# RetNet attention followed by a leaky-ReLU MLP: aligned tiles and a reordered first phase

## The chip, the cores and the metric

The kernel runs on one core of one Trainium2 chip. The metric is the device time of one execution in microseconds (us). The profile is one execution taken by the hardware profiler; its own times are counted from the first instruction.

## The reference

```python
# q, k, v: (8, 8, 576, 64); per head h, gamma = 1 - 2**(-5 - h)
scores = scale * np.matmul(q, k.transpose(0, 1, 3, 2))
Dmat = np.where(rel >= 0, gamma[:, None, None] ** rel[None, :, :], 0.0)   # rel = i - j
ret = np.matmul(scores * Dmat[None], v)
x = ret.transpose(0, 2, 1, 3).reshape(B * S, H * D)                        # 4608 x 512
h = x @ w_in                                                               # 512 x 2048
out = np.maximum(0.01 * h, h) @ w_out                                      # 2048 x 512
```

All inputs and the output are float32.

## The kernel before

**Tiling.** The 4608 tokens are cut into 36 units of 128 tokens, each of two chunks of 64. The attention runs in its recurrent form: for each unit, masked scores within a chunk, and a running state (k-transposed times v, summed over the chunks before) that serves all later chunks. The two wide products run over groups of 256 tokens (18 groups): a block of the first product (g1, `g1_blocks`, L408) is 8 matmuls of 128x256 into one PSUM bank and one Lrelu activation to float16 on ScalarE (L427); a block of the second (g2, `g2_blocks`, L434) is 4 matmuls of 128x512 (L443); after four of them VectorE copies the bank to `osb` (L453) and SP stores it. The first two groups' second product goes through four banks at once (`g2_wide`, L474, matmuls L488): rows n=0 and 1 in the pool `yps`, n=2 and 3 in the pool `hps`, which the first product uses too.

**A unit's steps.** `loads` (L133) brings q, k, v in float32. `casts` (L162) makes float16: k by ScalarE (L139), q and v times a decay table by VectorE or GpSimd (`scaled`, L141; VectorE for units below `NEARLY`). For units below `NPE` = 9, `transposes` (L169) turns q and k on TensorE (L179) and two copies bring them to SBUF (L185), k's on ScalarE, q's on VectorE; from unit 9 on, `cast_q` issues a DMA transpose on SP's queue (L153). `scores` (L191) computes the chunk scores (L198) and the state's increments (L207); `masks` (L214, VectorE L216) and `states` (L223, VectorE L230 to L240) follow; `state_copy` (L247, L249) makes a float16 state, by ScalarE for early units and by GpSimd after. `outputs_acc` (L257, units 0 to 3) or `outputs` (L290: ScalarE copy L319, VectorE addition L323) gives `xT`, the transposed input of the first product. `keep_warm` (L352) issues matmuls on zeros.

**Order.** The program is scheduled by hand: each engine runs its instructions in the order in which this code issues them. Up to about 68 us the order is written out line by line (L508 to L609); after that `run` (L463) spreads the `steady` steps (L372) evenly between blocks of g1 and g2. `steady(n)` does scores(n), outputs(n-1), masks(n), states(n), casts(n+3) and loads(n+5). Loads of units 0 to 11 and the weights are issued by GpSimd, which spends 0.88 us on each full load of a unit's q, k or v; the later loads, the DMA transposes from unit 9 on and the results are issued by SP, in order. `ld_pool` has five buffers for each of q, k and v, `h_pool` and `y_pool` two PSUM banks each, `sc_pool` and `ot_pool` one tile each. `sc_pool`'s tile serves scores and, from unit 4 on, the transposes.

In the written order the weights of the first product come in four quarters (two DMAs each, L337); the first block needs the first quarter.

```python
    blocks(0, 0)
    scores(3)
    outputs_acc(2)
    masks(3)
    states(3)
    blocks(0, 1)
...
    some(3, 4)
    casts(5)
    some(4, 6)
    outputs(4)
    transposes(5, sc_pool)
    some(6, 9)
    scores(5)
```

`blocks(g, fq)` is two blocks of g1; `some(a, b)` is wide blocks a to b-1 in the order part by part, n = 0 to 3 in each; `more(list, a, b)` is the same for g1[2] and g2.

Of the kernel before, what the change touches and what calls it, by code (L numbers as in the profile page):

```python
# [9 lines left out]
FP = mybir.dt.float32  # L10
F16 = mybir.dt.float16
# [6 lines left out]
def kernel(  # L18
# [23 lines left out]
    nc = tc.nc  # L42
# [3 lines left out]
    P = 128  # L46
# [26 lines left out]
    consts = np.concatenate([tab.reshape(P, -1), mask, gblk], axis=1).astype(np.float32)  # L73
# [4 lines left out]
    const_pool = ctx.enter_context(tc.tile_pool(name="const", bufs=1))  # L78
# [5 lines left out]
    sc_pool = ctx.enter_context(tc.tile_pool(name="scp", bufs=1, space=PSUM))  # L84
# [3 lines left out]

    ctx.enter_context(tc.manual_schedule())

    cs = const_pool.tile([P, consts.shape[1]], FP, name="cs")
    ident = const_pool.tile([P, P], F16, name="ident")
    nc.scalar.dma_start(out=cs, in_=c_dram.ap())
    nc.scalar.dma_start(out=ident, in_=i_dram.ap())
    tab_sb = cs[:, 0:NTAB].rearrange("p (w x h) -> p w x h", x=2, h=H)
# [7 lines left out]

    NPE = 9
    NFIRST = 8
    NEARLY = 9
    NRING = 11
    t32 = {}
    qk16 = {}
# [3 lines left out]
    st16 = {}  # L113
    st32 = {}
# [18 lines left out]
    def loads(u, eng):  # L133
        for x in (1, 0, 2):
            load(u, x, eng)
# [26 lines left out]
    def casts(u):  # L162
        if u >= NU:
            return
        cast_k(u)
        cast_q(u)
        cast_v(u)

    def transposes(u, pool=None):  # L169

        qkT[u] = b_pool.tile([P, 2, NP, P], F16, name="qkT")
        if pool is None:
            trs = [y_pool.tile([P, NP, P], F16, name="yps") for x in range(2)]
        else:
            both = pool.tile([P, 2, 2 * NP, P], F16, name="sc")
            trs = [both[:, x, 0:NP, :] for x in range(2)]
        for x in (1, 0):
            for p in range(NP):
                nc.tensor.transpose(  # L179
                    trs[x][:, p, :],  # L180
                    qk16[u][:, x, 2 * p : 2 * p + 2, :].rearrange("t h d -> t (h d)"),
                    ident,
                )
        for x in (1, 0):
            (nc.scalar.copy if x else nc.vector.tensor_copy)(  # L185
                out=qkT[u][:, x], in_=trs[x]
            )

# [34 lines left out]
    def states(u, copy=True):  # L223

        st = sc_tiles[u][:, :, 1]
        s32 = a_pool.tile([P, 2, NP, CH], FP, name="s32")
        st32[u] = s32
        for j, (b, c) in enumerate(units[u]):
            if c == CB - 1:
                nc.vector.memset(s32[:, j], 0.0)  # L230
                continue
            ends_block = c % CPB == CPB - 1
            dst = a_pool.tile([P, NP, CH], FP, name="stmp") if ends_block else s32[:, j]
            if c == 0:
                nc.vector.tensor_copy(out=dst, in_=st[:, j])
            else:
                prev = s32[:, 0] if j else st32[u - 1][:, 1]
                nc.vector.tensor_tensor(out=dst, in0=st[:, j], in1=prev, op=ADD)  # L238
            if ends_block:
                nc.vector.tensor_tensor(  # L240
                    out=s32[:, j], in0=dst,
                    in1=gblk_sb.unsqueeze(2).to_broadcast([P, NP, CH]), op=MUL,
                )
        if copy:
            state_copy(u)

    def state_copy(u):  # L247
        st16[u] = a_pool.tile([P, 2, NP, CH], F16, name="st16")
        (nc.scalar.copy if u < NEARLY else nc.gpsimd.tensor_copy)(out=st16[u], in_=st32[u])  # L249

    def st_before(u, j):

# [4 lines left out]
    def outputs_acc(u):  # L257

        ot = ot_pool.tile([P, 2, 2 * NP, CH], FP, name="ot")
        o_all = ot[:, 0].rearrange("q (c j) t -> q c j t", j=2)  # L260
        seen = set()
        for r in range(2):
            if r:
                nc.tensor.drain()
            for h in (0, 4, 1, 5, 2, 6, 3, 7):
                o, c = divmod(h, NP)
                nc.tensor.matmul(
                    out=o_all[half(o), c, r, :],
                    lhsT=v16[u][half(r), h, :],
                    rhs=s16s[u][half(r), h % 2, h // 2, :],  # L270
                    start=o not in seen, stop=False, skip_group_check=True,
                )
                seen.add(o)
            for j in range(2):
                if u == 0 and j == 0:
                    continue
                for h in (r, r + 4, r + 2, r + 6):
                    o, c = divmod(h, NP)
                    nc.tensor.matmul(
                        out=o_all[half(o), c, j, :],  # L280
                        lhsT=st_before(u, j)[half(r), h // 2, :],
                        rhs=qkT[u][half(r), 0, h // 2, half(j)],
                        start=False, stop=True, skip_group_check=True,
                    )
        t0 = P * u % XR
        nc.scalar.copy(
            out=xT[:, :, t0 : t0 + P], in_=o_all.rearrange("q c j t -> q c (j t)")
        )
# [53 lines left out]
            in_=moe_w_out[c * FQ : (c + 1) * FQ, :].rearrange("(c k) f -> k c f", k=P),  # L342
        )

    warm = const_pool.tile([P, 1], FP, name="warm")
    nc.vector.memset(warm, 0.0)
    nc.scalar.activation(out=warm, in_=warm, func=mybir.ActivationFunctionType.Lrelu)
    nc.vector.memset(zst, 0.0)
# [3 lines left out]
    def keep_warm(n):  # L352

        t = h_pool.tile([P, 1, TOK], FP, name="hps")
        for _ in range(n):
            nc.tensor.matmul(out=t[:, 0, :], lhsT=idle[:, 0:P], rhs=idle, start=True, stop=True)
# [36 lines left out]
    ends = []  # L393
# [69 lines left out]
    def run(upto, *lists):  # L463

        order = sorted(
            ((n + 0.5) / len(ls), x, n) for x, ls in enumerate(lists) for n in range(len(ls))
        )
        a = done
        for m, (_, x, n) in enumerate(order):
            lists[x][n]()  # L470
            run_steps(min(upto, a + -(-(upto - a) * (m + 1) // max(1, len(order) - 3)), done + 1))
        run_steps(upto)

    def g2_wide(tbs):  # L474


        ys = []

        def block(part, n):
            g, tb = tbs[n]  # L480
            for f in range(4 * part, 4 * part + 4):
                if f == 0:
                    ys.append(
                        y_pool.tile([P, DM], FP, name="yps")
                        if n < 2
                        else h_pool.tile([P, 1, DM], FP, name="hps")[:, 0, :]
                    )
                nc.tensor.matmul(  # L488
                    out=ys[n],
                    lhsT=g_tiles[g][:, f, tb * P : (tb + 1) * P],  # L490
                    rhs=w_out16[:, f, :],
                    start=(f == 0),
                    stop=(f == NF - 1),
                )
            if part == 3:
                osb = o_pool.tile([P, DM], FP, name="osb")
                nc.vector.tensor_copy(out=osb, in_=ys[n])  # L497
                r0 = starts[g] + tb * P
                nc.sync.dma_start(out=out[r0 : r0 + P, :], in_=osb)

        return [lambda part=part, n=n: block(part, n) for part in range(4) for n in range(4)]

    def blocks(g, *parts):
        for fq in parts:
            for m in (2 * fq, 2 * fq + 1):
                g1[g][m]()

    g1 = [g1_blocks(g) for g in range(3)]  # L508
# [11 lines left out]
    for u in (2, 3):  # L520
# [8 lines left out]
        states(u - 1)  # L529
        if u == 2:  # L530
            cast_v(3)
    blocks(0, 0)
    scores(3)
    outputs_acc(2)
    masks(3)
    states(3)
    blocks(0, 1)
    outputs_acc(3)
    blocks(0, 2)
# [1 line left out]
    loads(5, nc.gpsimd)  # L541
    for c in (2, 3):
        load_w_out(c)
    for u in range(6, NRING + 1):
        loads(u, nc.gpsimd)
    blocks(1, 1)
    blocks(1, 2)
    blocks(0, 3)
    casts(4)
    blocks(1, 3)  # L550

    wide = g2_wide([(0, 0), (0, 1), (1, 0), (1, 1)])
# [1 line left out]
    def some(a, b):  # L554
        for m in range(a, b):
            wide[m]()

    g2 = g2_blocks(2)

    def more(blocks, a, b):  # L560
        for m in range(a, b):
            blocks[m]()

    some(0, 1)
    transposes(4, sc_pool)
    some(1, 3)
    scores(4)
    masks(4)
    states(4)
    some(3, 4)  # L570
    casts(5)
    some(4, 6)
    outputs(4)
    transposes(5, sc_pool)
    some(6, 9)
    scores(5)
    masks(5)
    states(5)
    some(9, 13)
    outputs(5)  # L580
    some(13, 14)
    casts(6)
    some(14, 16)
    transposes(6, sc_pool)
    more(g1[2], 0, 2)
    scores(6)
    masks(6)
    states(6, copy=False)
    more(g1[2], 2, 3)
    state_copy(6)  # L590
    casts(7)
    more(g1[2], 3, 5)
    outputs(6)
    transposes(7, sc_pool)
    more(g1[2], 5, 7)
    scores(7)
    masks(7)
    states(7, copy=False)
    more(g1[2], 7, 8)
    more(g2, 0, 1)  # L600
    state_copy(7)
    casts(8)
    more(g2, 1, 3)
    outputs(7)
    casts(9)
    loads(12, nc.sync)
    transposes(8, sc_pool)
    casts(10)
    more(g2, 3, 4)  # L609
    run(ends[4], g1_blocks(3), g2[4:])  # L610
    for g in range(4, NG):
        run(ends[g + 1], g1_blocks(g), g2_blocks(g - 1))
    g2 = g2_blocks(NG - 1)
# [44 lines left out]
```

## Time and profile before

| what | value |
|---|---|
| runs | 308.23, 308.55, 312.86, 312.96, 314.57 us (median 312.86) |
| profiled execution | 308.23 us, span 306.3 us |
| granted TensorE clock over the span | 0.998 |
| time before the first block of the first product | 19.18 us |
| loads of q, k, v by GpSimd, by SP | 256 KB each, median 4.9 to 5.1 us and 3.4 to 4.2 us from issue to landing |
| w_in quarters | two DMAs each, 9.0 us median from issue to landing |
| DMA transposes | 27 on SP's queue, 2.8 us median to landing |

PE is TensorE, DVE VectorE, ACT ScalarE, POOL GpSimd and SP SyncE; "SPq" and "POOLq" are issues of DMAs. A timeline row has the start, the duration, the engine, the line, the operation with its output and inputs, how many instructions were merged, and in brackets how long the engine had been idle and what ended that. A stage row has the length, then busy time and instruction count for PE, PEld (weight loads), DVE, ACT and POOL, the granted clock, the DMA engines' share and GB/s. PE ends are modelled, so that neighbouring PE rows overlap by some tenths.

### The profile page before, as it was taken

Reading aid. Unit: us, or ns where it says so; the run is one execution under the profiler, and the core shown is the slowest. Engines: PE = TensorE matmul, PEld = TensorE weight load, DVE = VectorE, ACT = ScalarE, POOL = GpSimd, SP = SyncE. Lnnn points to the kernel's source line nnn. Section 1 sums busy time; section 2 is a strip of 40 time slices with the busy share of each in tenths; the row PEclk is TensorE's granted clock in tenths of the full one; section 3 lists DMA queues with packets and bytes.
Section 4 is the critical chain, followed back from the end, with each engine's and each line's share of the span. In section 5 each row is a group of like instructions: output and inputs, shape, how many; then the busy total and the mean of one; then the engine's idle time right before and its main releaser. Section 6 shows DMA issues by size and latency. Waiting matters only on the chain.

```text
span 306.3 us, 9346 instructions
## 1 busy us (share of the span) xinstructions
PE 291.1 (95%) x4122; PEld 196.8 (64%) x4122; DVE 116.0 (38%) x222; ACT 136.9 (45%) x237; POOL 112.2 (37%) x135
## 2 busy tenths in 40 slices
PE   1889999998999999999999999999999999999995
PEld 0568754765666666666666666666666666666653
DVE  2760246664443324243434333333434233331001
ACT  4366623666453535353535353535353534343320
POOL 8944949800633333333333333333333330000000
PEclk9999999999999999999999999999999999999999
DMA  7999999709899884959795957676767620100111
GB/s 201 249 197 243 223 276 318 243 5 199 191 240 202 223 189 138 201 145 198 130 211 153 205 144 176 170 166 181 170 177 170 175 71 36 36 36 34 44 61 68
DMA packets 117368, 49.73 MB, mean 162 GB/s; under 512 B 106128, under 2 KB 110608, under 8 KB 117328
## 3 DMA queue, kind: packets, MB, share of 16 engines
q1 hardware_dynamic: 109760, 35.60, 49.1%
q0 software_dynamic: 7136, 13.37, 18.5%
q8 instruction: 32, 0.52, 0.8%
q10 hardware_dynamic: 432, 0.17, 0.2%
q14 instruction: 8, 0.07, 0.1%
HBM read 36.81 MB, written 9.44 MB: 151 GB/s over the span
## 4 chain that ended last, share of the span: by engine, by line
PE 85%; POOL 3%; DMA 3%; DVE 3%; SPq 2%; ACT 1%; issue 1%; ACTq 0%; POOLq 0%
PE hps L420 38%; PE yps L443 35%; POOL t L129 3%; PE sc L198 3%; DMA w_in<-in_moe_w_in_dram 2%; PE yps L488 2%; PE hps L488 2%; SPq L153 1%; PE ot L300 1%; PE sc L207 1%; PE ot L311 1%; PE yps L618 1%; DMA t<-in_k_dram 1%; PE sc L179 1%; ACT gt L427 0%
## 5 line engine op out<-in xcount | busy, mean ns | idle before, releaser
L420 PE MATMUL hps<-xT,w_in 128*128 128x256 f16 x1152 | 145.9, 273 | 1.4 <-DVE osb L497 0.7
L427 ACT ACTIVATE gt<-hps 128x512 f16<-128x512 f32 x144 | 85.6, 597 | 123.0 <-PE hps L420 122.7
L420 PEld LDWEIGHTS <-w_in 128*128 128x128 f16 x1152 | 112.3, 98 | 40.1 <-issue 2.6
L443 PE MATMUL yps<-w_out,gt 128*128 128x512 f16 x496 | 126.6, 380 | 0.0
L249 POOL CAST st<-s 128x512 f16<-128x512 f32 x27 | 16.5, 612 | 145.5 <-DVE s L238 80.0
L443 PEld LDWEIGHTS <-gt 128*128 128x128 f16 x496 | 46.1, 98 | 33.9
L323 DVE TENSOR_TENSOR xT<-ot,own 128x512 f16<-128x512 f32 x32 | 22.1, 692 | 79.5 <-ACT own L319 79.5
L453 DVE COPY osb<-yps 128x512 f32<-128x512 f32 x31 | 21.2, 685 | 73.5 <-PE yps L443 73.5
L142 POOL TENSOR_TENSOR qk<-t,cs 128x512 f16<-128x512 f32 x27 | 28.7, 1062 | 0.7 <-DMA t<-in_q_dram 0.5
L142 POOL TENSOR_TENSOR v<-t,cs 128x512 f16<-128x512 f32 x27 | 28.4, 1050 | 0.7 <-DMA t<-in_v_dram 0.7
L216 DVE TENSOR_TENSOR s<-sc,cs 128x512 f16<-128x512 f32 x36 | 24.6, 683 | 8.1 <-PE sc L207 8.0
L139 ACT CAST qk<-t 128x512 f16<-128x512 f32 x36 | 22.3, 620 | 7.2 <-DMA t<-in_k_dram 7.1
L319 ACT COPY own<-ot 128x512 f32<-128x512 f32 x32 | 18.7, 586 | 8.9 <-PE ot L311 7.0
L238 DVE TENSOR_TENSOR s<-sc,s 128x256 f32<-128x256 f32 x40 | 16.8, 420 | 0.7
L198 PEld LDWEIGHTS <-qkT 64*64 64x64 f16 x576 | 7.7, 109 | 9.7 <-issue 6.7
L198 PE MATMUL sc<-qkT 64*64 64x64 f16 x576 | 11.7, 200 | 1.7 <-DMA qkT<-qk 1.6
L129 POOL DMA_DIRECT2D t<-in_q_dram x13 | 11.4, 874 | 4.4 <-DMA t<-in_k_dram 2.3
L129 POOL DMA_DIRECT2D t<-in_k_dram x12 | 10.3, 862 | 5.1 <-ACT gt L427 2.0
L179 PEld LDWEIGHTS <-qk 128*128 128x128 f16 x72 | 5.2, 111 | 10.8 <-ACT qk L139 7.1
L179 PE MATMUL yps<-ident,qk 128*128 128x128 f16 x32 | 4.1, 287 | 8.1 <-ACT qk L139 6.0
L129 POOL DMA_DIRECT2D t<-in_v_dram x13 | 11.2, 861 | 1.3 <-DMA w_in<-in_moe_w_in_dram 1.2
L142 DVE TENSOR_TENSOR qk<-t,cs 128x512 f16<-128x512 f32 x9 | 6.6, 728 | 13.2 <-DMA t<-in_q_dram 13.2
(44 smaller groups left out, 153.6 us busy)
## 6 DMA issues: line engine op xcount, KB each, us to landing
out_dram<-osb SPq DMA_DIRECT2D x35, 256.0 KB, 3.7
t<-in_k_dram SPq DMA_DIRECT2D x22, 256.0 KB, 3.4
t<-in_q_dram SPq DMA_DIRECT2D x21, 256.0 KB, 3.8
t<-in_v_dram SPq DMA_DIRECT2D x21, 256.0 KB, 4.2
t<-in_q_dram POOLq DMA_DIRECT2D x11, 256.0 KB, 4.9
t<-in_v_dram POOLq DMA_DIRECT2D x11, 256.0 KB, 5.1
t<-in_k_dram POOLq DMA_DIRECT2D x10, 256.0 KB, 5.1
w_in<-in_moe_w_in_dram POOLq DMA_DIRECT2D x8, 256.0 KB, 9.0
```

The lines of the kernel that those rows point to most:

```text
L129: eng.dma_start(out=dst, in_=src[b, :, CH * c : CH * c + n, :].rearrange("h t d -> t h d"))
L139: nc.scalar.copy(out=qk16[u][:, 1], in_=t32[u, 1])
L142: (nc.vector if u < NEARLY else nc.gpsimd).tensor_tensor(out=out, in0=t32[u, x], in1=tab_sb[:, kind(u), x // 2, :].unsqueeze(2).to_broadca ...
L198: nc.tensor.matmul(out=a[half(j), g, 0, p, :], lhsT=qkT[u][half(g), 1, p, half(j)], rhs=qkT[u][half(g), 0, p, half(j)], start=True, stop=T ...
L216: nc.vector.tensor_tensor(out=s16s[u], in0=sc_tiles[u][:, :, 0], in1=mask_sb.unsqueeze(1).unsqueeze(1).to_broadcast([P, 2, NP, CH]), op=MUL,)
L238: nc.vector.tensor_tensor(out=dst, in0=st[:, j], in1=prev, op=ADD)
L319: nc.scalar.copy(out=tmp.rearrange("q c (j t) -> q c j t", t=CH), in_=own.rearrange("q j c t -> q c j t"),)
L323: nc.vector.tensor_tensor(out=xT[:, :, t0 : t0 + P].rearrange("q (s g) t -> q g s t", g=2), in0=far, in1=tmp.rearrange("q (s g) t -> q g s ...
L420: nc.tensor.matmul(out=hps[:, f, :], lhsT=w_in16[:, c, fc * P : (fc + 1) * P], rhs=xT[:, c, t0 % XR : t0 % XR + tok], start=(c == 0), stop ...
L427: nc.scalar.activation(out=g_tiles[g][:, fb * nf : (fb + 1) * nf, :], in_=hps, func=mybir.ActivationFunctionType.Lrelu,)
L443: nc.tensor.matmul(out=y_cur[g, tb], lhsT=g_tiles[g][:, f, tb * P : (tb + 1) * P], rhs=w_out16[:, f, :], start=(f == 0), stop=(f == NF - 1),)
L453: nc.vector.tensor_copy(out=osb, in_=y_cur[g, tb])
```

## The change

Five things change together.

1. Sizes of the constant tiles: a pad of 96 floats comes first, `cs`, `ident` and `warm` are rounded up, so that each SBUF tile begins at a multiple of 512 bytes. Before, `cs`, `ident`, `xT`, `w_in16`, `w_out16`, `zst` and `warm` did not.
2. `NEARLY` goes from 9 to 6: q and v of units 6, 7 and 8 are cast by GpSimd. The state copies stay on ScalarE up to unit 7 (`NACT` = 8); unit 8's goes to GpSimd.
3. The q copies of the transposes of units 0 to 3 go from VectorE to ScalarE; so do the copies to `osb` of the wide rows n=2 and 3.
4. Three more `keep_warm` matmuls come after unit 1's outputs, then the first block, then scores(3), masks(3), states(3), then the second block, then outputs_acc(2).
5. In the written order, casts(4) to casts(10), transposes(4) to (7), outputs and loads(9) to (12) move between blocks; loads(9), (10), (11) now alternate with the casts of units 6, 7 and 8 in GpSimd's queue, casts(9) and (10) follow, and one more g2 block of group 2 precedes the `run` steps.

```diff
-    cs = const_pool.tile([P, consts.shape[1]], FP, name="cs")
-    ident = const_pool.tile([P, P], F16, name="ident")
+    const_pool.tile([P, 96], FP, name="pad")
+    cs_all = const_pool.tile([P, 256], FP, name="cs")
+    cs = cs_all[:, 0 : consts.shape[1]]
+    ident_all = const_pool.tile([P, 2 * P], F16, name="ident")
+    ident = ident_all[:, 0:P]
...
-    NEARLY = 9
+    NEARLY = 6
+    NACT = 8
...
-            (nc.scalar.copy if x else nc.vector.tensor_copy)(
+            (nc.scalar.copy if x or u < 4 else nc.vector.tensor_copy)(
...
-        (nc.scalar.copy if u < NEARLY else nc.gpsimd.tensor_copy)(out=st16[u], in_=st32[u])
+        (nc.scalar.copy if u < NACT else nc.gpsimd.tensor_copy)(out=st16[u], in_=st32[u])
...
-    warm = const_pool.tile([P, 1], FP, name="warm")
+    warm = const_pool.tile([P, P], FP, name="warm")[:, 0:1]
...
-                nc.vector.tensor_copy(out=osb, in_=ys[n])
+                (nc.vector.tensor_copy if n < 2 else nc.scalar.copy)(out=osb, in_=ys[n])
...
-    blocks(0, 0)
+    keep_warm(3)
+    g1[0][0]()
     scores(3)
-    outputs_acc(2)
     masks(3)
     states(3)
+    g1[0][1]()
+    outputs_acc(2)
     blocks(0, 1)
...
-    for u in range(6, NRING + 1):
+    for u in (6, 7, 8):
         loads(u, nc.gpsimd)
     blocks(1, 1)
     blocks(1, 2)
+    casts(4)
     blocks(0, 3)
-    casts(4)
     blocks(1, 3)
...
-    some(0, 1)
+    some(0, 2)
     transposes(4, sc_pool)
-    some(1, 3)
+    some(2, 5)
     scores(4)
     masks(4)
     states(4)
-    some(3, 4)
+    some(5, 6)
     casts(5)
-    some(4, 6)
+    transposes(5, sc_pool)
+    some(6, 8)
     outputs(4)
-    transposes(5, sc_pool)
-    some(6, 9)
+    some(8, 9)
     scores(5)
     masks(5)
     states(5)
-    some(9, 13)
+    loads(9, nc.gpsimd)
+    casts(6)
+    some(9, 12)
+    loads(10, nc.gpsimd)
+    casts(7)
+    some(12, 13)
     outputs(5)
     some(13, 14)
-    casts(6)
+    transposes(6, sc_pool)
     some(14, 16)
-    transposes(6, sc_pool)
-    more(g1[2], 0, 2)
+    more(g1[2], 0, 1)
     scores(6)
     masks(6)
     states(6, copy=False)
-    more(g1[2], 2, 3)
+    loads(11, nc.gpsimd)
+    casts(8)
+    more(g1[2], 1, 3)
     state_copy(6)
-    casts(7)
-    more(g1[2], 3, 5)
+    more(g1[2], 3, 4)
+    transposes(7, sc_pool)
+    more(g1[2], 4, 5)
     outputs(6)
-    transposes(7, sc_pool)
+    casts(9)
     more(g1[2], 5, 7)
     scores(7)
     masks(7)
     states(7, copy=False)
     more(g1[2], 7, 8)
-    more(g2, 0, 1)
     state_copy(7)
-    casts(8)
-    more(g2, 1, 3)
+    casts(10)
+    loads(12, nc.sync)
+    more(g2, 0, 2)
     outputs(7)
-    casts(9)
-    loads(12, nc.sync)
+    more(g2, 2, 3)
     transposes(8, sc_pool)
-    casts(10)
-    more(g2, 3, 4)
-    run(ends[4], g1_blocks(3), g2[4:])
+    more(g2, 3, 5)
+    run(ends[4], g1_blocks(3), g2[5:])
```

## The prediction

> **What bounds the kernel now.** I read the page's busy shares first, then busy times by stage, the chain of work that ended last, and the timeline where that chain leaves TensorE.
>
> ```profile
> span 306.3 us, 9346 instructions
> PE 291.1 (95%) x4122; PEld 196.8 (64%) x4122; DVE 116.0 (38%) x222; ACT 136.9 (45%) x237; POOL 112.2 (37%) x135
> ```
>
> TensorE (PE) is busy 95% of the span and no other engine half of it. Stage by stage (length, then PE busy):
>
> ```profile
> 35.40:53.35 17.95, 17.25 (x218) 8.66 (x216) 9.16 (x18) 5.78 (x11) 13.58 (x17) 1.00 1.06 277
> 53.35:84.00 30.65, 28.18 (x537) 20.43 (x537) 17.07 (x32) 18.11 (x33) 12.66 (x13) 1.00 0.68 160
> 84.00:120.00 36.00, 36.00 (x491) 24.27 (x493) 13.45 (x26) 16.37 (x28) 12.57 (x16) 1.00 0.91 205
> 120.00:200.00 80.00, 80.00 (x1201) 54.21 (x1201) 29.86 (x57) 37.12 (x64) 26.94 (x31) 1.00 0.76 172
> 200.00:295.00 95.00, 95.00 (x1217) 64.40 (x1216) 29.52 (x56) 38.83 (x67) 20.15 (x24) 1.00 0.40 105
> ```
>
> From 84 to 295 us PE never waits and the granted clock is 1.00: nothing that this change does to other engines can shorten that. What can move lies before 84 us. The chain:
>
> ```profile
> 11.70 7.34 DMA w_in<-in_moe_w_in_dram
> 19.18 1.91 PE hps L420 x16
> 71.33 1.98 SPq L153
> 77.24 2.87 DMA t<-in_k_dram
> 87.50 0.86 PE yps L443 x4
> 88.36 0.87 PE hps L420 x8
> ```
>
> The first real matmul waits for w_in until 19.18; later the chain leaves PE for a DMA transpose (L153) and a load of k. A block of the first product (8 matmuls) costs 0.87, of the second (4) 0.86. The places that the sum uses, in the timeline:
>
> ```profile
> 23.50 0.62 ACT L249 CAST st<-s 128x512 f16<-128x512 f32 x1 [0.65 <-DVE s L240]
> ...
> 38.53 0.32 PE L198 MATMUL sc<-qkT 64*64 64x64 f16 x16
> ...
> 40.38 0.62 ACT L249 CAST st<-s 128x512 f16<-128x512 f32 x1 [2.88 <-DVE s L235]
> ...
> 40.90 0.61 ACT L139 CAST qk<-t 128x512 f16<-128x512 f32 x1
> ...
> 41.98 0.62 PE L179 MATMUL sc<-ident,qk 128*128 128x128 f16 x8
> ```
>
> Unit 5's k is cast 2.5 us after unit 4's scores end (38.98 to 41.51); PE has three wide blocks and outputs(4) to do meanwhile.
>
> ```profile
> 53.35 1.91 PE L420 MATMUL hps<-xT,w_in 128*128 128x256 f16 x16 [0.71 <-DVE osb L497]
> ...
> 59.01 1.53 POOL L142 TENSOR_TENSOR qk<-t,cs 128x512 f16<-128x512 f32 x1 [0.52 <-DMA t<-in_q_dram]
> ...
> 75.93 0.61 POOL L249 CAST st<-s 128x512 f16<-128x512 f32 x1 [14.10 <-DVE s L238]
> ...
> 76.80 0.32 PE L198 MATMUL sc<-qkT 64*64 64x64 f16 x16 [1.63 <-DMA qkT<-qk]
> ...
> 80.21 0.62 ACT L139 CAST qk<-t 128x512 f16<-128x512 f32 x1 [1.87 <-DMA t<-in_k_dram]
> ```
>
> PE's waits after 19.18: 0.9 at 52.46 (the evacuation of a bank by VectorE, L497), about 1.05 between 53.35 and 67.6 (12 blocks of 0.87, two scores and two outputs of 0.47 and two transposes of 0.45 make 13.2; it took 14.25), 1.55 at 75.2, 0.5 at 80.9 (an activation behind the k cast of 80.21). Together 4.0: that is the most that can be won there.
>
> **The change, part by part.**
>
> Tiles on 512 bytes. In the built programs only cs, ident, xT, w_in16, w_out16, zst and warm stood off a 512-byte line; all loads, casts, states and results already stood on one. The rows tell what that cost: 4 matmuls that stream w_out16 take 0.86 and 8 that stream xT take 0.87, the same time per column, and weights from w_in16 load in 98 ns as those from the aligned gt do. So PE: 0. A faster landing of w_in could save at most 0.5 (landed 19.05, PE free at 18.63). Bounds -0.5 to 0; I take 0, since new warm-up matmuls fill that gap.
>
> keep_warm(3) ahead of the first block: 3 x 0.216 from 18.63 ends at 19.28, 0.1 after the start before. +0.1 (0 to 0.65, the latter if w_in lands early).
>
> Copies of early transposes on ScalarE: four copies of 0.42 leave VectorE, four of 0.59 join ScalarE's queue. Units 0 to 2 are covered: the next cast of k there waits for its load or PE comes 2 us later (scores(2) at 16.65, copies done 14.6). Unit 3's pushes the xT copy from 18.09 to 18.3, done 18.9, under the 19.05 of w_in. 0 (0 to 0.2).
>
> First block, then scores(3), then the second block. A scores group between wide matmuls costs 0.47 (38.44 to 38.91), beside outputs_acc 0.24. And ScalarE now holds state_copy(3) ahead of the second block's activation. Before, scores(3) began 21.02 and the state copy 23.50, 2.48 later; now scores begin at 19.28+0.87+0.1=20.25, the copy at 22.73, done 23.35, the activation done 23.95. PE has done the second block, outputs_acc(2) (0.89) and the third by 23.25 and needs that bank for the fourth: it waits 0.7. Against 24.91 before, the end of outputs_acc(3) comes at 23.95+0.87+0.89=25.7: +0.8 for the whole start, the 0.1 included (bounds +0.3, +1.1).
>
> casts(4) two blocks earlier: 0.61 of ScalarE between activations that leave it 0.28 a block: +0.1 (0 to 0.3).
>
> transposes(5) moved ahead of outputs(4) and of two wide blocks. Behind scores(4) PE has one block (0.86) and a switch, so it is there 1.0 after the scores' end, while k is cast 2.53 after it: mask, state, state copy and cast stand in line, as at 38.98 to 41.51. PE waits 1.6, and everything behind it in its queue. +1.6 (1.0 to 1.9).
>
> osb of two banks on ScalarE, casts(6) off VectorE: the bank is free 0.7 after its matmuls, under the last wide block of 0.86. -0.9 (-0.9 to -0.5). The two stores behind these copies now wait for ScalarE on SP's queue; next on it is transposes(9) at 62, so that costs 0. transposes(4) comes a block later: its copies take 1.2, and three blocks (2.6) still stand before scores(4): 0.
>
> Casts of units 6 to 8 on GpSimd between load issues: six casts of 1.05 for six of 0.69 on VectorE. GpSimd issues loads(9) until 48.47 as now, casts 6 to 50.6, loads(10) (3 x 0.88) to 53.25, q and v of unit 7 to 55.35, loads(11) to 58.0, then units 8, 9, 10 to 64.3. Behind each cast queue the next three load issues; loads(10) and (11) go out 2.1 and 4.2 later, and who reads them (k casts of 10 and 11) comes after 65. PE wants q of unit 6 at about 52.8 (ready 49.6), of 7 at 58.9 (54.3), of 8 at 67 (59). Hidden, with 3 to 8 us to spare. The row of 59.01 shows such a cast at 1.53 beside VectorE's casts: three of those before q(7) would add 1.5, still hidden. The Trainium skill's "SBUF — State Buffer", section "SBUF: two separate sides", speaks against the move: VectorE and GpSimd share a port pair as an exclusive lock, and the loser blocks for the whole instruction. By it each moved cast could wait out one VectorE cast of 0.69, some 2 us by q(7), so the sum would stay; the slowed 1.53 agrees in direction.
>
> 53 to 67 us: with k casts 7 and 8 early and VectorE lighter, I follow g1[2] block by block and find one wait of 0.27 (an activation behind own and k of unit 9) in place of 1.05: -0.8 (-1.0 to 0).
>
> 67 to 84 us: transposes(9) and (10) on SP's queue go out at 62 and 66 instead of 67.51 and 71.33, ahead of loads(12), so the 1.55 at 75.2 loses its cause. What is late next: outputs(9) wants unit 9's state, which GpSimd had only at 76.54 (75.93+0.61), 4.8 after scores(9). That is almost as late. Also steady(9) follows steady(8) after two blocks instead of three, and unit 8's state copy is now GpSimd's: outputs(8) waits 0.5. I get outputs(9) done at 77.6 against 77.44. Coming in 0.8 late, that is -0.7 (-1.5 to +0.5). The 0.5 at 80.9 stays: loads(13) still stands behind transposes(11), whose q GpSimd casts after that state copy, at 74.3 against 74.09.
>
> Sum: 0.8 + 0.1 + 1.6 - 0.9 - 0.8 - 0.7 = +0.1 us on the profiled execution's 308.23 (span 306.3 and 1.9 around it): 308.3. That execution is the lowest of five (308.55 next); the median shown, 312.86, is 4.6 higher, for no reason that this profile shows. I put the forecast where its two low runs lie, 308.4 + 0.1 = 308.5.
>
> **The rivals.**
>
> Faster: transposes(5) does not wait and the start costs nothing, so only gains stay: -0.9 -0.8 -1.5 = -3.2, 305.3. For it: the waits removed stand in the trace. Against: the cast of k(5) is in line behind state_copy(4), 2.5 us of measured work.
>
> Slower: GpSimd becomes the bound at transposes(7). It decides once q(7) is over 4.5 us late. Casts doubled to 2.1 and one more wait for a DMA slot as before the issue at 44.09 (2.25) make 3.2+2.25=5.4: +0.9 at that place on top of the sum, 309.4; each further wait of that size puts its full 2.25 on PE, 311.7. Against: loads(5) to (8), where such waits stood, are issued as before.
>
> The alignment acts where no row shows it: 1% on the two wide products (about 233 us of PE) is 2.3 either way, 306.2 or 310.8.
>
> **How the numbers follow.** Forecast 0.58, faster rival 0.20, slower rival 0.13, alignment 0.09. The range takes the faster rival's 305.0 at the low end; at the high end the slower rival, and the spread of the runs shown, 313.5. The forecast's own range is 307 to 310. Two per cent, about what a measurement of this kernel can tell from no change, is 6.3 of 312.86: below 306.6 is faster, above 319.1 slower. The faster rival and the good half of the alignment (0.20 + 0.05) reach 306.6 only if the runs do not scatter upwards as three of five did before; about half of that is 0.13. Slower needs three or more GpSimd waits and that scatter, or a place that I did not see: 0.07. Within: 0.80.
>
> **What would show it.** A wait of about 1.6 at the transposes of unit 5, none before the first block of g1[2], the fourth block waiting for an activation near 23.5, first matmul at 19.3, no wait for a qkT transpose near 76 but one for a GpSimd state, paces of 0.86 and 0.87 unchanged. A different pace between 84 and 295 us, or GpSimd named as releaser at transposes(7), would make it wrong.

## The result: 0.7% slower, and the profile after

The changed kernel takes 312.24 us (median of 43 runs, 309.71 to 316.80), the kernel before 310.13 us (median of 80, 307.23 to 315.69): a ratio of 1.0072, interval 1.0053 to 1.0090, or 2.2 us more. The profiled execution took 314.40 us and spent one stretch at half clock; so the first experiment's profile (the same order of work, 310.38 us, full clock throughout) is read beside it.

Span and totals, then five stages, from the changed kernel's page and busy times by stage (columns: start:end, length, busy time of PE, PEld, DVE, ACT, POOL, granted clock, DMA share, GB/s):

```profile
span 312.4 us, 9349 instructions
PE 293.1 (94%) x4125; PEld 196.9 (63%) x4125; DVE 112.1 (36%) x210; ACT 139.5 (45%) x242; POOL 118.3 (38%) x142
```

```profile
19.71:36.78 17.07, 16.54 (x225) 13.91 (x226) 3.26 (x6) 10.85 (x19) 11.46 (x15) 1.00 1.17 233
36.78:55.65 18.87, 17.25 (x219) 8.53 (x216) 7.83 (x15) 6.91 (x12) 15.29 (x18) 1.00 0.98 256
...
90.00:126.00 36.00, 36.00 (x493) 24.27 (x484) 13.45 (x26) 16.34 (x29) 12.15 (x15) 1.00 0.78 181
```

The last row reads as it did before: from there to the end PE never waits, and the stage from g1[4] to g1[5] takes 15.38 to 15.39 in both kernels. Only the part before g1[4], the first block of group 4, differs. Its stages, each from the start of one block to the start of the next named:

| stage | before | changed | changed with the old tile sizes (e1) | best (e9) |
|---|---|---|---|---|
| first block to first wide block | 16.22 | 17.07 | 17.07 | 16.33 |
| first wide block to g1[2] | 17.95 | 18.87 | 18.86 | 17.51 |
| g1[2] to g1[3] | 14.34 | 16.26 | 14.13 | 14.13 |
| g1[3] to g1[4] | 14.56 | 16.48 | 14.54 | 12.52 |

One g2 block, 0.86 us, changed stages: between g1[2] and g1[3] PE has 16 matmuls of g2 before and 20 after, and four fewer in the next. For equal work, e1's third stage is 14.13 - 0.86 - 14.34 = -1.07, and its fourth 14.54 + 0.86 - 14.56 = +0.84. Added up, e1 loses 0.85 + 0.91 - 1.07 + 0.84 = 1.53.

PE's waits (engine, line, what it waited for: us in total, times, longest) of the changed kernel up to 100 us:

```profile
PE hps L425 <- ACT gt L432: 2.7, 2, 2.3
PE sc L184 <- DVE s L243: 2.0, 1, 2.0
PE sc L184 <- ACT qk L144: 1.6, 1, 1.6
```

And the places, in its timeline:

```profile
44.00 0.61 ACT L144 CAST qk<-t 128x512 f16<-128x512 f32 x1
44.67 0.62 PE L184 MATMUL sc<-ident,qk 128*128 128x128 f16 x8 [1.62 <-ACT qk L144]
...
57.91 1.06 POOL L147 TENSOR_TENSOR qk<-t,cs 128x512 f16<-128x512 f32 x1
58.18 3.07 DVE L245 TENSOR_TENSOR s<-stmp,cs 128x256 f32<-128x256 f32 x1
58.91 1.05 POOL L147 TENSOR_TENSOR v<-t,cs 128x512 f16<-128x512 f32 x1
59.92 1.04 POOL L147 TENSOR_TENSOR qk<-t,cs 128x512 f16<-128x512 f32 x1
60.92 1.23 POOL L147 TENSOR_TENSOR v<-t,cs 128x512 f16<-128x512 f32 x1
61.29 0.42 DVE L243 TENSOR_TENSOR s<-sc,s 128x256 f32<-128x256 f32 x1
61.76 0.61 PE L184 MATMUL sc<-ident,qk 128*128 128x128 f16 x8 [1.98 <-DVE s L243]
...
83.08 0.62 ACT L144 CAST qk<-t 128x512 f16<-128x512 f32 x1 [2.32 <-DMA t<-in_k_dram]
84.25 1.87 PE L425 MATMUL hps<-xT,w_in 128*128 128x256 f16 x8 [2.33 <-ACT gt L432]
```

Three waits: transposes(5) behind the k cast of unit 5 (1.62, foreseen); transposes(7) behind a VectorE product that took 3.07 where the same line took 0.84 before; and a g1 block behind an activation that itself stood behind the k cast of unit 13, whose load had not landed (2.33). The two waits before at g1[2] and at a qkT are gone. The 8 matmuls of 84.25 took 1.87, where such a row at full clock reads 1.03 to 1.05. Stages around it:

```profile
80.70:84.00 3.30, 1.22 (x12) 0.95 (x10) 2.47 (x5) 0.98 (x3) 1.57 (x3) 1.00 0.79 179
84.00:87.40 3.40, 3.15 (x12) 1.76 (x12) 0.00 (x0) 1.28 (x3) 2.19 (x3) 0.50 0.98 211
87.40:90.80 3.40, 3.40 (x85) 2.47 (x84) 0.69 (x1) 1.68 (x4) 0.00 (x0) 1.00 1.24 196
```

For 3.4 us from the end of that wait on the granted clock is 0.50: half the work, 1.7 us lost by estimate.

### The profile page after: what moved, and what is told of

Same layout as the page of the kernel before. It is cut to its first block, busy times and chain, and to the rows that moved or that the text cites. A ratio compares the mean times of both kernels' runs of the same rounds, so it can differ in the third digit from the quotient of the medians.

```text
span 312.4 us, 9349 instructions
## 1 busy us (share of the span) xinstructions
PE 293.1 (94%) x4125; PEld 196.9 (63%) x4125; DVE 112.1 (36%) x210; ACT 139.5 (45%) x242; POOL 118.3 (38%) x142
## 4 chain that ended last, share of the span: by engine, by line
PE 87%; DVE 3%; POOL 3%; DMA 2%; ACT 2%; issue 1%; SPq 1%; ACTq 0%; POOLq 0%
PE hps L425 38%; PE yps L448 35%; PE sc L203 3%; PE hps L493 2%; PE yps L493 2%; POOL t L134 2%; PE ot L305 1%; DMA t<-in_q_dram 1%; PE sc L212 1%; PE ot L316 1%; DVE s L245 1%; PE yps L630 1%; DMA t<-in_k_dram 1%; DVE s L221 1%; PE sc L184 1%
## 5 line engine op out<-in xcount | busy, mean ns | idle before, releaser
L425 PE MATMUL hps<-xT,w_in 128*128 128x256 f16 x1152 | 147.5, 274 | 3.8 <-ACT gt L432 2.7
L147 POOL TENSOR_TENSOR v<-t,cs 128x512 f16<-128x512 f32 x30 | 31.5, 1050 | 0.4 <-DMA t<-in_v_dram 0.4
L147 POOL TENSOR_TENSOR qk<-t,cs 128x512 f16<-128x512 f32 x30 | 31.3, 1044 | 0.3
L221 DVE TENSOR_TENSOR s<-sc,cs 128x512 f16<-128x512 f32 x36 | 24.6, 684 | 9.3 <-PE sc L212 9.3
L243 DVE TENSOR_TENSOR s<-sc,s 128x256 f32<-128x256 f32 x40 | 16.8, 420 | 0.7
L212 PE MATMUL sc<-v,qk 64*64 64x64 f16 x576 | 10.8, 194 | 0.0
```

The costliest lines, as they stand in the source:

```text
L147: (nc.vector if u < NEARLY else nc.gpsimd).tensor_tensor(out=out, in0=t32[u, x], in1=tab_sb[:, kind(u), x // 2, :].unsqueeze(2).to_broadca ...
L221: nc.vector.tensor_tensor(out=s16s[u], in0=sc_tiles[u][:, :, 0], in1=mask_sb.unsqueeze(1).unsqueeze(1).to_broadcast([P, 2, NP, CH]), op=MUL,)
L425: nc.tensor.matmul(out=hps[:, f, :], lhsT=w_in16[:, c, fc * P : (fc + 1) * P], rhs=xT[:, c, t0 % XR : t0 % XR + tok], start=(c == 0), stop ...
```

## The experiments

Ratios are to the kernel before, run on the same chip, with 95% intervals. Stage lengths come from one profile each.

**e1: the tiles' old sizes back in the changed kernel.**

```diff
-    const_pool.tile([P, 96], FP, name="pad")
-    cs_all = const_pool.tile([P, 256], FP, name="cs")
-    cs = cs_all[:, 0 : consts.shape[1]]
-    ident_all = const_pool.tile([P, 2 * P], F16, name="ident")
-    ident = ident_all[:, 0:P]
+    cs = const_pool.tile([P, consts.shape[1]], FP, name="cs")
+    ident = const_pool.tile([P, P], F16, name="ident")
...
-    warm = const_pool.tile([P, P], FP, name="warm")[:, 0:1]
+    warm = const_pool.tile([P, 1], FP, name="warm")
```

> The changed kernel with the tile sizes of before (xT, w_in16, w_out16 off the 512-byte lines again), all else as changed. Theory (the loss of 0.7% comes from waits that the new order makes): nothing moves, ratio to before 1.005 to 1.009, the wide products at 0.86 and 0.87 us a block, the same four waits. Rival (the new tile places cost or give something): a pace other than 0.86 and 0.87 between 100 and 290 us, or a ratio off by more than 0.3% from 1.007.

Measured 1.0105 (1.0053 to 1.0157; 6 runs): no better than the change itself. From 100 to 290 us PE is busy throughout without the alignment (190.00 of 190 us) as it is with it, and of the three waits the first and the last are there. Alignment is not the loss, and no gain from it shows. In its stages and timeline:

```profile
55.73:69.86 14.13, 14.13 (x230) 10.10 (x229) 6.44 (x12) 9.86 (x18) 10.75 (x12) 1.00 0.81 191
69.86:84.40 14.54, 12.14 (x237) 8.89 (x236) 7.07 (x15) 6.68 (x12) 7.80 (x9) 1.00 0.79 182
100.00:290.00 190.00, 190.00 (x2698) 128.80 (x2696) 67.00 (x128) 83.40 (x143) 54.10 (x63) 1.00 0.60 145
```

```profile
73.23 0.61 POOL L251 CAST st<-s 128x512 f16<-128x512 f32 x1 [6.72 <-PE hps L422]
73.81 1.04 POOL L144 TENSOR_TENSOR qk<-t,cs 128x512 f16<-128x512 f32 x1
...
74.87 1.49 SPq L155 DMA_TRANSPOSE qkT<-qk  x1
...
76.46 1.39 SPq L131 DMA_DIRECT2D t<-in_k_dram  x2
...
80.63 0.62 ACT L141 CAST qk<-t 128x512 f16<-128x512 f32 x1 [1.93 <-DMA t<-in_k_dram]
...
81.80 1.03 PE L422 MATMUL hps<-xT,w_in 128*128 128x256 f16 x8 [1.93 <-ACT gt L429]
```

Here PE works through the third stage without a wait, and in the fourth its one long wait (1.93) ends the chain of the second fence: GpSimd's copy of unit 8's state, the q cast of unit 11 behind it, the transposes of unit 11, the load of k 13 behind them on SP, its landing, the cast, the activation, PE.

**e2: transposes(5) where they were.**

```diff
-    transposes(5, sc_pool)
     some(6, 8)
     outputs(4)
+    transposes(5, sc_pool)
     some(8, 9)
```

> The changed kernel with transposes(5) back behind two wide blocks and outputs(4). Theory: the wait of 1.62 us at 44.67, for the k cast of unit 5 behind state_copy(4), goes, and the time falls by some 1.6 us: ratio 1.002. Rival (later steps are set by loads and casts and take it back): the wait goes, but the waits near 61 and 84 us grow by as much: ratio stays near 1.007.

Measured 1.0020 (0.9991 to 1.0049; 12 runs). The wait of 1.62 is gone and the second stage is 17.52, 1.35 shorter. The ratio is 0.5% under the change's, though the two intervals lie close together (0.9991 to 1.0049, 1.0053 to 1.0090). Its profile still waits 2.28 at the k cast of unit 13 and has a half-clock stretch behind it.

**e3: q and v of units 6 to 8 on VectorE again.**

```diff
-    NEARLY = 6
+    NEARLY = 9
```

> The changed kernel with q and v of units 6 to 8 cast on VectorE again, in the changed places of the order; the load issues stay between them. Theory: the VectorE product of 3.07 us at 58.18 (0.42 elsewhere) was held off by GpSimd casts back to back, and the 1.98 us wait of transposes(7) came from it: with four fewer casts in that train, the product takes under 1.3 us, the wait is under 0.5, ratio about 1.001. Rival (it was a chance of that run, or VectorE is too busy with its own casts): the wait at transposes(7) stays over 1 us or comes back before the scores: ratio 1.005 or more.

Measured 1.0073 (1.0039 to 1.0107; 10 runs). In the profile the product of L245 takes 0.61 and transposes(7) do not wait. But GpSimd runs casts back to back at that place here too, those of units 9 and 10, and the product starts amid them and ends between two:

```profile
56.69 1.04 POOL L147 TENSOR_TENSOR v<-t,cs 128x512 f16<-128x512 f32 x1
...
57.42 0.61 DVE L245 TENSOR_TENSOR s<-stmp,cs 128x256 f32<-128x256 f32 x1
57.69 1.23 POOL L147 TENSOR_TENSOR qk<-t,cs 128x512 f16<-128x512 f32 x1
```

So the short product does not come from a missing run of casts, and the time did not fall. The 2 us wait of the changed kernel's profile is hardly what its median pays: e1, e2 and e5 hold the same casts on GpSimd, and there the product took 0.88, 0.67 and 0.49.

**e5: unit 8's state copy on ScalarE again.**

```diff
-    NACT = 8
+    NACT = 9
```

> The changed kernel with unit 8's state copy on ScalarE again, so that GpSimd casts q of unit 11 without waiting for it. Theory: the DMA transpose of unit 11 (76.93) and with it the loads of unit 13 (78.88) go out 2 to 3 us earlier, the k cast of unit 13 comes in time, and the wait of 2.33 us at 84.25 shrinks under 0.7; the half clock that follows it in some runs (84.3 to 87.7, 1.7 us) goes too: ratio 0.998 to 1.002. Rival (the loads of unit 13 are late for the whole shift of the order, not for this copy): ratio stays over 1.005 and the wait over 1.5.

Measured 1.0054 (1.0016 to 1.0093; 12 runs), not to be told from the change. The transposes of unit 11 did not go out 2 to 3 us earlier:

```profile
73.57 0.62 ACT L254 CAST st<-s 128x512 f16<-128x512 f32 x1 [1.65 <-DVE s L235]
74.09 0.61 ACT L144 CAST qk<-t 128x512 f16<-128x512 f32 x1
...
74.78 1.86 SPq L158 DMA_TRANSPOSE qkT<-qk  x1
...
76.75 1.39 SPq L134 DMA_DIRECT2D t<-in_k_dram  x2
...
80.91 0.62 ACT L144 CAST qk<-t 128x512 f16<-128x512 f32 x1 [1.36 <-DMA t<-in_k_dram]
```

They were issued at 74.78, where e1 had 74.87. They need both q and k of unit 11. In e1 the q cast behind GpSimd's state copy ends last (73.81 and 1.04 later). In e5 GpSimd has cast unit 11 by 68.5, and now the k cast behind ScalarE's state copy ends last (74.09 and 0.61 later). So the copy of unit 8's state stands ahead of one of the two casts either way: e5 moved it from one chain into the other, and does not show that the copy holds nothing up.

**e4: the start as before.**

```diff
-    keep_warm(3)
-    g1[0][0]()
+    blocks(0, 0)
     scores(3)
+    outputs_acc(2)
     masks(3)
     states(3)
-    g1[0][1]()
-    outputs_acc(2)
```

> The changed kernel with the start as before: no extra warm-up matmuls, both first blocks ahead of scores(3), outputs_acc(2) right behind. Theory: from the first block to the first wide block it took 16.22 us before and 17.07 changed, for the second block's activation behind state_copy(3); this goes back to about 16.3. Behind it PE arrives 0.8 earlier, but the k cast of unit 13 near 80.5 is set by SP's loads, so most of that is given back there: ratio 1.004 to 1.007. Rival (the start counts in full): ratio 1.007 less 0.003, with the wait behind the k cast unchanged at about 1.9 us.

Measured 1.0028 (0.9994 to 1.0062; 12 runs). The first stage is 16.33 instead of 17.07: the reordered start costs 0.74 in this profile. The wait at the k cast of unit 13 stays (1.7).

**e6: in every `steady` step, the loads ahead of the casts.** SP's queue then holds the loads of unit n+5 before the DMA transposes of unit n+3.

```diff
-            casts(n + 3)
             if n + 5 < NU:
                 loads(n + 5, nc.sync)
+            casts(n + 3)
```

> The changed kernel with the loads of a steady step issued on SP ahead of its DMA transpose, so that loads(13) no longer stand behind the transpose of unit 11. Theory: what the changed order wins before 76 us is given back at one place, where ScalarE's k cast of unit 13 waits for that load (80.6) and the activations behind it hold PE for 1.9 to 2.4 us; with the load issued some 2 us earlier or more, this wait falls under 0.7, and windows of half clock become rarer (24 of 44 runs of the changed kernel were under 0.996): ratio 1.000 to 1.003. Rival (the load is late for another reason, a buffer or the DMA engines): the wait stays over 1.5 and the ratio at 1.007.

Measured 1.0025 (0.9993 to 1.0058; 12 runs). The fourth stage falls from 14.54 (e1) to 12.53, the largest single step of all stages; the ratio is 0.5% under the change's:

```profile
74.63 1.42 SPq L134 DMA_DIRECT2D t<-in_k_dram  x2
...
79.48 1.26 SPq L158 DMA_TRANSPOSE qkT<-qk  x1
...
80.29 0.62 ACT L144 CAST qk<-t 128x512 f16<-128x512 f32 x1
```

The load of k 13 goes out at 74.63, ahead of the transposes of unit 11 (79.48), and the cast starts without a wait. This profile happened to hold the long product:

```profile
57.52 3.36 DVE L245 TENSOR_TENSOR s<-stmp,cs 128x256 f32<-128x256 f32 x1
```

With it the third stage took 16.55. The 10 runs at full clock lie in two groups, 308.05 to 308.95 (five) and 310.00 to 311.22 (five, the profiled one among them); that this product parts them is likely but not shown, since only one was profiled.

**e7: e2, e4 and e6 together; e9: the same with the three warm-up matmuls kept; e11: e7 with the old tile sizes; e10: e7 with the casts on VectorE (NEARLY = 9).** e9's edit on e7:

```diff
+    keep_warm(3)
     blocks(0, 0)
     scores(3)
```

> The changed kernel with three places mended at once: the start as before, transposes(5) behind two wide blocks and outputs(4), loads ahead of casts in the steady steps. Theory (three places make the loss, the rest of the change is a gain): 0.85 + 1.35 + 1.9 us less than the changed kernel, some 2 us under before: ratio 0.990 to 0.996. Rival (the next chain behind takes it back, for instance GpSimd's state copy of unit 9 or the DMA transposes, which now stand behind six loads): ratio 0.998 or more, with a new wait of over 1 us between 70 and 90 us.

> The mended kernel (start as before, transposes(5) late, loads first) with the three extra warm-up matmuls kept ahead of the two first blocks. Theory: they cost 0 to 0.3 us, since the first block waits for w_in until 19.2 anyway, and keep PE from the idle stretch that gave the mended kernel's profile a window of half clock from 19.5 (1.7 us): same ratio as the mended kernel at full clock, 0.990 to 0.993, and no run whose half clock begins near 19.5. Rival: the warm-up delays the first block whenever w_in is early, ratio 0.994 or more.

> The mended kernel with the tile sizes of before. Theory: tiles on 512 bytes do nothing: ratio 0.989 to 0.993, blocks of 0.86 and 0.87 us. Rival (they give a little that the waits of the changed kernel hid): ratio 0.994 or more.

> The mended kernel with q and v of units 6 to 8 cast on VectorE again. Theory (the casts on GpSimd were hidden either way, and VectorE was not what PE waited for): ratio within 0.2% of the mended kernel's 0.991. Rival (the casts on GpSimd were the gain of the change): ratio 0.994 or more, with PE waiting for VectorE between 50 and 68 us.

| kernel | median us (runs) | ratio to before | interval |
|---|---|---|---|
| e7 | 306.20 (6) | 0.9913 | 0.9883 to 0.9943 |
| e9 | 306.33 (6) | 0.9906 | 0.9879 to 0.9933 |
| e11 | 306.19 (6) | 0.9908 | 0.9877 to 0.9940 |
| e10 | 307.13 (12) | 0.9939 | 0.9912 to 0.9966 |

All four beat both kernels. e9's stages:

```profile
19.56:35.89 16.33, 16.16 (x225) 13.93 (x226) 3.26 (x6) 10.86 (x19) 10.17 (x14) 1.00 1.17 236
35.89:53.40 17.51, 17.14 (x218) 8.72 (x216) 7.74 (x15) 6.82 (x12) 14.36 (x17) 1.00 1.02 265
53.40:67.53 14.13, 14.13 (x230) 10.13 (x229) 6.15 (x12) 9.98 (x18) 10.47 (x11) 1.00 0.81 189
67.53:80.05 12.52, 12.06 (x237) 8.90 (x236) 7.07 (x15) 6.69 (x12) 6.17 (x8) 1.00 1.06 206
```

Against before they give 0.11 - 0.44 - 1.07 - 1.18 = -2.6 us (the last two for equal work); the ratio says -2.9. e11 says once more that alignment does nothing that its interval of 0.3% either way can show. e7's profile has a half-clock stretch behind the wait for w_in; none of e9's 6 runs has a mean clock under 0.997, against 2 of e7's 6, too few runs to say that the warm-up did it. e10's long product (2.63, and a wait of 1.5 at transposes(7)) came although units 6 to 8 were on VectorE: it fell in the run of casts of the units after them, at 54.34 to 58.38. Whether VectorE casts cost the 0.3% between e10 and e7, the intervals don't tell.

**e8: the kernel before, with the two `osb` copies on ScalarE and the loads ahead of the casts.**

```diff
-            casts(n + 3)
             if n + 5 < NU:
                 loads(n + 5, nc.sync)
+            casts(n + 3)
...
-                nc.vector.tensor_copy(out=osb, in_=ys[n])
+                (nc.vector.tensor_copy if n < 2 else nc.scalar.copy)(out=osb, in_=ys[n])
```

> The kernel before with two things alone: the osb copies of the wide rows n=2 and 3 on ScalarE, and loads ahead of casts in the steady steps. Theory: the wait of 0.71 at 53.35 goes, and the 0.5 behind the k cast at 80.21; the wait of 1.63 for the DMA transpose of unit 10 at 76.80 stays: ratio 0.996. Rival (ScalarE is late there, or the transposes are later behind the loads): ratio 0.999 or more.

Measured 0.9974 (0.9949 to 0.9999; 12 runs), with its theory's 0.996 inside the interval. In its profile the second stage is 17.08 instead of 17.95 and the fourth 14.11 instead of 14.56, but the wait of 1.63 for a qkT stays, at 78.97, and the third stage grew from 14.34 to 15.21: there PE waits 1.01 for a state copied behind the same product of VectorE, which took 1.71. No variant of the changed kernel has the wait for a qkT, and all hold the earlier casts and transposes of units 9 and 10. That these moves removed it, and are what is good in the change, fits the rows, but no run tests them alone.

**e12: GpSimd's casts of unit 8 put between the loads of unit 11, in the changed kernel.**

```diff
-    loads(11, nc.gpsimd)
-    casts(8)
+    load(11, 1, nc.gpsimd)
+    cast_k(8)
+    cast_q(8)
+    load(11, 0, nc.gpsimd)
+    cast_v(8)
+    load(11, 2, nc.gpsimd)
```

> The changed kernel with unit 8's casts between the single load issues of unit 11, instead of behind all three, so that GpSimd runs at most one cast at a time there. Theory: VectorE's product of two SBUF operands (3.07 and 3.36 us in two profiles, 0.42 elsewhere) waits while casts run back to back; between single casts it gets in after at most one, under 1.6 us, transposes(7) waits under 0.6, and the time falls by the mean share of that wait: ratio 1.002 to 1.007. Rival (load issues hold VectorE off as casts do): the product stays over 2 us where it meets them, ratio 1.007 or more.

Measured 1.0059 (1.0033 to 1.0085; 12 runs), within the changed kernel's interval. The product has a gap to start in:

```profile
56.96 1.05 POOL L147 TENSOR_TENSOR v<-t,cs 128x512 f16<-128x512 f32 x1
...
57.63 0.75 DVE L245 TENSOR_TENSOR s<-stmp,cs 128x256 f32<-128x256 f32 x1
57.95 0.92 POOL L134 DMA_DIRECT2D t<-in_v_dram  x1
```

It starts within one cast and ends in 0.75, before the load's issue (57.95) is over. One profile does not show that the long product is gone. Load issues are not free of the effect either: in e4 and e7 the product ran beside load issues alone and took 1.28 and 1.15, in e2 and e5 0.67 and 0.49.

## Why the prediction was wrong, point by point

The forecast was no change (+0.1 us, 308.5), and the runs resolve a slowdown of 2.2 us. Of the 3.7 us between 308.5 and 312.24, 1.7 is the base: I put it at 308.4, by the two low runs of five, and the median of 80 runs is 310.13. That 312.24 lies in the range is luck: the range's high end was taken from the spread of the five runs shown, while the forecast's own range ended at 310 and the slower rival's sum, for another cause, at 311.7. (At the low end the range has 305.0 where the faster rival's sum gives 305.3.)

- **Start, +0.8:** right in size. The first stage is 17.07 instead of 16.22 (+0.85); e4 gives back 0.74. The wait for the activation came at the fourth block as drawn, but took 0.35 and not 0.7; the rest is not put down to a row. The first block itself starts at 18.60 to 19.80 from profile to profile with the changed start and at 19.17 to 19.71 with the old one; the 0.1 for the warm-up can't be seen in that.
- **transposes(5), +1.6, and `osb`, -0.9:** right. The wait was 1.62, the one at g1[2] is gone. With casts(4) at +0.1 the first two stages were forecast at +1.6 and measured +1.77. e2 removes 1.35.
- **53 to 67 us, -0.8:** right in direction; for equal work -1.07 at full clock (e1), a little past the bound of -1.0, since the wait of 0.27 that I had left in did not come.
- **67 to 84 us, -0.7: this step failed.** It gave +0.84 in e1, outside its bounds of -1.5 to +0.5. The parts that I worked out came true: the wait of 1.55 for a qkT lost its cause, GpSimd's late state cost 0.21 where I had 0.5, and outputs(9) were done at 77.94 in e1 for the 77.6 drawn. What failed is "The 0.5 at 80.9 stays". I carried that wait over as a fixed amount because its load would go out at the same time (76.46 in e1, 76.47 before: that was right). But it is the rest between a chain and the work that PE has meanwhile. From the start of scores(8) to the k cast of unit 13 the chain (casts, DMA transposes, load, landing) took 11.56 before and still 9.81 in e1. PE's path from there to the block that waits got shorter by more. Two g2 blocks and one g1 block fewer stand in it (g2 at 69.03, 72.39, 77.44 and 80.06 before, at 71.20 and 75.84 in e1), 2.6 us by the paces of 0.86 and 0.87, since one g2 block now precedes the `run` steps, which space the rest otherwise; and the removed wait stood in it too (1.63 in its row, 1.55 in my sum). The ends of both paths, before and in e1:

```profile
68.65 0.32 PE L198 MATMUL sc<-qkT 64*64 64x64 f16 x16
...
81.38 1.91 PE L420 MATMUL hps<-xT,w_in 128*128 128x256 f16 x16 [0.28 <-ACT gt L427]
```

```profile
70.82 0.32 PE L200 MATMUL sc<-qkT 64*64 64x64 f16 x16
...
81.80 1.03 PE L422 MATMUL hps<-xT,w_in 128*128 128x256 f16 x8 [1.93 <-ACT gt L429]
```

The chain lost 1.75. PE's path lost 2.6 and 1.63, less 0.45 of new short waits (0.21 and 0.24) and 0.4 because two groups of scores and outputs took 0.84 where they took 0.65: 3.4 in all. The difference, 1.65, is what the last wait grew by, from 0.28 in its row (0.5 in my sum, by the paces of the blocks) to 1.93. So the removed wait came back at the next place, with the time of the moved blocks on top. I had read that steady(9) follows steady(8) sooner and had drawn it for outputs(8) only. e6 settles it: with the load ahead of the transposes the fourth stage is 2.0 shorter and the cast doesn't wait; in e9, where that holds too, the stage is 1.18 shorter than before for equal work, within the bounds.

- **GpSimd's casts hidden:** right for their own outputs: no wait of PE on q or v of units 6 to 8, and GpSimd's rows came as drawn (unit 8's casts from 57.91, 58.0 drawn). The slower rival named transposes(7) with q late; PE did wait there in the changed kernel's profile, but for VectorE. The Trainium skill's "SBUF — State Buffer", section "SBUF: two separate sides", which I cited with GpSimd as the loser, says of the lock that whichever instruction starts first has the pair for its whole length. Here it was VectorE that lost, 3.07 for 0.84, a cost that I had put at nothing. e3 (1.0073) and e12 (1.0059) did not bring the time down clear of the change's interval, so it is hardly in the median.
- **Alignment, 0:** right (e1, e11).

What adds up: in e1, at full clock, the terms add to +1.53, where I had +0.1; the fourth stage alone is off by 1.54. The executions with a mean clock of 0.997 or more have a median of 310.64 for the changed kernel (20 of 44) and of 308.74 for the kernel before (49 of the 80 that ran beside the experiments; its runs of the result have no clock on record), +1.9. Run beside the kernel before on one chip, at such clocks, two variants that are not to be told from the change lie +1.9 (e1, 2 runs) and +1.6 (e12, 8 runs) above it. The rest up to 2.2 may be the half-clock stretches: 24 of those 44 had one, and 31 of those 80. At 1.7 us each that is 0.16 x 1.7 = 0.3, an estimate, since the two sets did not run together. How often VectorE's long product occurs, and so what it is worth on average, stays open: only profiled runs show it, and three of the twelve of the changed kernel and its variants did.

## What to carry to other kernels

A wait that "stays" is not a constant: write it as the length of the chain behind it minus what the waiting engine has in between, its work and its other waits, and work out both anew whenever blocks move. Where an in-order queue holds a load behind something that waits for compute, try first to issue the load ahead of it: here that swap was worth 2.0 us of stage time, about as much as the change lost. A reordering that removes one wait shows its worth only when the next one is removed too: as written these moves lost 0.7%; with the start and transposes(5) put back and the loads ahead of the casts they won 0.9%.

## What the runs showed of the hardware that was not expected

**Half clock after short waits.** After a PE wait of 1.2 us (e7, at the first block) and of 2.3 us (changed kernel, e2) the granted clock was 0.50 for 3.4 us; in e8 it was 0.51 from 19.70 to 23.10, after a wait of 1.3 for w_in. e7's timeline has the wait and the slow block (16 matmuls in 3.33; 1.91 at full clock):

```profile
19.17 3.33 PE L425 MATMUL hps<-xT,w_in 128*128 128x256 f16 x16 [1.17 <-DMA w_in<-in_moe_w_in_dram]
```

Waits of 1.93 (e1) and 2.4 (e3) left the clock at full speed. The Trainium skill's "TensorE: Matmul & The Clock Gate", section "HAM oscillation — how this bites in real kernels", gives the rule as no gaps of PE over some 3.4 us; here 1.2 and 2.3 were enough in some executions, so the measurement decides: a wait of 2 us cost 1.7 more in some of them. What decides whether it does is not settled by these runs.

**One product held off through several casts.** A VectorE product with both inputs in SBUF took 2.63 to 3.36 in three profiles in which GpSimd ran casts of 1.05 back to back, 0.49 to 1.71 at this place in the others, and 0.42 or 0.43 in every later step. In the changed kernel it did not get in between two casts at first: it began 0.27 after the first had begun and ended 0.33 after the fourth had. The products on either side of it, with one input in PSUM (L243, L221), took their usual 0.42 and 0.69. The lock as told above is held for one instruction; here the product waited through three casts, and in e6 its row begins at 57.52, 0.03 ahead of the first cast's, and lasts 3.36 all the same. What decides it is not settled: amid casts back to back it took 0.84 (before) and 0.61 (e3) when it began 0.49 and 0.73 after a cast's start, but 2.63 (e10) when it began 0.69 after one's.
